# Linear attention and a SwiGLU block on one core: v ahead of the first weights, fewer dummy matmuls, q's casts on two engines

## The chip, the cores and the metric

The kernel runs on one core of one Trainium2 chip. The metric is the device time of one execution in microseconds (us); smaller is better. The tensor engine (TensorE) is called PE below. VectorE is DVE, ScalarE is ACT, GpSimd is POOL, SyncE is SP. POOL issues the loads, and SP issues the first load of q and most of the stores.

## The reference

```python
# q, k, v: (8 batches, 8 heads, 576 positions, 64); phi(x) = elu(x) + 1
kv  = einsum('bhsd,bhse->bhde', phi(k), v);  z = sum over s of phi(k)
x   = einsum('bhsd,bhde->bhse', phi(q), kv) / (einsum('bhsd,bhd->bhs', phi(q), z) + 1e-6)
# heads side by side: x becomes (4608 tokens, 512)
out = (silu(x @ w_gate) * (x @ w_val)) @ w_out        # w_gate, w_val 512 x 1536; w_out 1536 x 512
```

## The kernel before

The work is nine groups of 512 tokens. For each group PE runs layer 1 (96 matmuls of 512 columns, line 290) and layer 2 (48 of them, line 297); attention for the next batches is slipped in between. The attention of batch 0 has nothing to hide behind. It is a chain of short steps at the start, and dummy matmuls (`warm`) fill PE's waits so that its clock rises. That chain, and the order of the first loads, are what the change touches. In the code, `kv` is summed up by PE in PSUM (the tiles named `pp`) and copied out as R; Zr is the same for z. The `corners` are the small matmuls of R and Zr with phi(q): with R they give the numerators of x, with Zr the denominators.

```python
    WARM = (34, 14, 16, 7, 3, 3, 2)
    # [cut]
    def warm(n, w=1, ps=None):      # n dummies of 128*w columns; each is a weight load and a matmul
        for _ in range(n):
            nc.tensor.matmul(out=(ps or pp4[2][1])[:, 256:256 + P * w], lhsT=ones[:, :],
                             rhs=ones[:, :].unsqueeze(1).to_broadcast([P, w, P]), start=True, stop=True)
    # [cut]  kv_corner: 36 matmuls of 64x64; corners: 4 matmuls of up to 512 columns; zt: 9 of 2 columns
    nc.sync.dma_start(out=q32[:, :, :], in_=q[0]...[:, 0:2, :])    # half of q, fp32, quick queue
    ld(q, qr, 0, 1)                                                # the other half, cast by the DMA
    ld2(k, kr, 0)
    ld(v, vr, 0, 0)
    ld_w1(0, 256, 0, 2)
    ld(v, vr, 0, 1)
    ld_w1(0, 256, 2, 4)
    # [cut]  more weights, then:
    ld_w2(0, 4); ld(q, qr, 1, 0); ld_w2(4, 8); ld(q, qr, 1, 1); ld_w2(8, 12); ld2(v, vr, 1)
    # [cut]  the chain, in the order of the program
    for l in range(2):
        nc.vector.tensor_copy(out=qr[0][:, l, :], in_=q32[:, l, :])
    warm(WARM[0])
    for lp in range(2):
        qtr(0, lp, pq[lp])          # 16 transposes of q on PE
        warm(WARM[1 + lp])
        ph[lp][0]()                 # exp on ACT
    # [cut]  exp, max, min of k; z matmuls (zt); Zr; first Zr corners; first k.v; R copy
    zr_copy(0, 1, pp4[3][1])
    warm(WARM[5], 2, pp4[1][1])
    t_corners(0, R, 0, pp4[0])      # numerators of the first four heads
    x_t(0, 0, pp4[0], (0,))         # DVE multiplies: x
    t_corners(0, Zr, 1, pp4[3])     # denominators of the other four heads
    lnrd(pp4[3], 1)
    x_t(0, 0, pp4[0], (1,))
    warm(WARM[6], 2, pp4[1][1])
    l1_mm(0, 0, pp4[2], (0,))
    kv_corner(0, 1, kp, True, False)   # second k.v
    kv_corner(0, 1, ek, False, True)
    r_copy(0, 1, 2, "VV")
    l1_mm(0, 1, pp4[0], (0,))
    t_corners(0, R, 1, pp4[1])
    x_t(0, 1, pp4[1])
    for c in (1, 2, 3):             # twelve layer-1 matmuls without a break
        l1_mm(0, 0, pp4[2], (c,)); l1_mm(0, 1, pp4[0], (c,))
```

Much later, near 81 us, the block for batch 2 issues 144 small k.v matmuls at once and then corners:

```python
            kv_all(b1); r_copy(b1, 0, 2, "AA"); kv_all(b2)        # 2 x 72 matmuls of 64x64
            for lp in range(2):
                corners(kvp[b2], Zr[1], 1, lp, 7, 9, 2 * P + P * lp)
            lnrd(kvp[b2], 0, 2 * P, 4 * P)                        # on ACT
            for lp in range(2):
                num(b1, lp)                                       # R corners
                # [cut]
```

Of the kernel before, what the change touches and what calls it, by code (L numbers as in the profile page):

```python
# [17 lines left out]
def kernel(  # L18
# [10 lines left out]
    nc = tc.nc  # L29
# [10 lines left out]
    EPS = 1e-6  # L40
    SC = 4096.0
    NB = 3
    WARM = (34, 14, 16, 7, 3, 3, 2)

    sb = ctx.enter_context(tc.tile_pool(name="sb", bufs=1))
    pp = ctx.enter_context(tc.tile_pool(name="ps", bufs=1, space=bass.MemoryType.PSUM))
# [2 lines left out]
    def many(shape, dt, name, n=2):  # L49
        return [sb.tile(shape, dt, name=f"{name}_{i}") for i in range(n)]  # L50

    kr = many([P, HL, J * D], FP16, "kr", NB)
    qr = many([P, HL, J * D], FP16, "qr", NB)
    vr = many([P, HL, J * D], FP16, "vr", NB)
# [5 lines left out]
    R = many([P, 2, 2, D], FP16, "R", 3)  # L60
# [4 lines left out]
    q32 = sb.tile([P, 2, J * D], FP32, name="q32")  # L65
# [22 lines left out]
    pp4 = [[pp.tile([P, 512], FP32, name=f"pp_{2 * i + e}") for e in range(2)] for i in range(4)]  # L88
# [11 lines left out]
    def ld(src, dst, b, lp):  # L100
        nc.gpsimd.dma_start(out=dst[b % NB][:, 2 * lp:2 * lp + 2, :],  # L101
                            in_=src[b].rearrange("(l a) (c j) d -> (a c) l (j d)", a=2, j=J)[:, 2 * lp:2 * lp + 2, :])

    def ld2(src, dst, b):
        ld(src, dst, b, 0)
        ld(src, dst, b, 1)

    def ld_w1(f0, f1, c0=0, c1=4):
        for (src, dst) in ((moe_w_gate, wg), (moe_w_val, wv)):
            nc.gpsimd.dma_start(out=dst[:, c0:c1, f0:f1],  # L110
                                in_=src[P * c0:P * c1, f0:f1].rearrange("(c p) f -> p c f", p=P))
# [5 lines left out]
    def act(out, in_, func=AF.Copy, scale=1.0, bias=0.0):  # L117
        nc.scalar.activation(out=out, in_=in_, func=func, bias=bias, scale=scale)  # L118

    def warm(n, w=1, ps=None):  # L120
# [3 lines that stand above are left out]
# [53 lines left out]
    def kv_corner(b, lp, t, first, last):  # L177
        ps = kvp[b]
        for j in range(J):
            for l2 in range(2):  # L180
                for hh in range(2):
                    rows = slice(C * hh, C * hh + C)
                    nc.tensor.matmul(out=ps[hh][D * l2:D * l2 + D, D * lp:D * lp + D],  # L183
                                     lhsT=t[b % 2][rows, lp, j, D * l2:D * l2 + D],
                                     rhs=vr[b % NB][rows, 2 * lp + l2, D * j:D * j + D],
                                     start=(first and j == 0), stop=(last and j == J - 1))
# [6 lines left out]
    def r_copy(b, l0, l1, engs):  # L193
        for hh in range(2):
            src = kvp[b][hh][:, D * l0:D * l1].rearrange("p (l d) -> p l d", d=D)
            if engs[hh] == "A":
                act(R[b % 3][:, l0:l1, hh, :], src)
            else:
                nc.vector.tensor_copy(out=R[b % 3][:, l0:l1, hh, :], in_=src)
# [38 lines left out]
    def units(g):  # L238
        us = [(u // J, u % J) for u in range(U * g, U * g + U)]
        res = []  # L240
        for b in sorted(set(u[0] for u in us)):
            js = [j for (bb, j) in us if bb == b]
            res.append((b, js[0], js[-1] + 1, C * us.index((b, js[0]))))
        return us, res
# [3 lines left out]
    def corners(ps, W, b, lp, j0, j1, c0):  # L248
        for l2 in range(2):
            rows = slice(D * l2, D * l2 + D)  # L250
            for hh in range(2):
                nc.tensor.matmul(out=ps[l2][C * hh:C * hh + C, c0:c0 + C * (j1 - j0)],  # L252
                                 lhsT=W[rows, lp, hh, :], rhs=qt(b, lp, hh, j0, j1)[rows],
                                 start=True, stop=True)
# [16 lines left out]
    def l1_mm(g, fb, ps, chunks):  # L271
        for c in chunks:
            for h, w in enumerate((wg, wv)):
                nc.tensor.matmul(out=ps[h][:, :], lhsT=w[:, c, P * fb:P * fb + P], rhs=xT[g % 2][:, c, :],  # L274
                                 start=(c == 0), stop=(c == 3))
# [36 lines left out]
    def l2_out(g, t, eng, n0=0, n1=512, o=None):  # L312
# [8 lines left out]
        for e in range(2):  # L321
# [9 lines left out]
                      in_=q[0].rearrange("(l a) (c j) d -> (a c) l (j d)", a=2, j=J)[:, 0:2, :])  # L331
    ld(q, qr, 0, 1)
    nc.gpsimd.iota(out=idx[:, :], pattern=[[-1, P]], base=0, channel_multiplier=1)
    ld2(k, kr, 0)
    ld(v, vr, 0, 0)
    ld_w1(0, 256, 0, 2)
    ld(v, vr, 0, 1)
    ld_w1(0, 256, 2, 4)
    ld_w1(256, 512)
    ld_w1(512, 768)  # L340
# [23 lines left out]
    def qtr(b, lp, ps):  # L364
        pt = ps[:, :].bitcast(FP16).rearrange("p (j c) -> p j c", c=P)
        for j in range(J - 1):
            for l2 in range(2):
                nc.tensor.transpose(out=pt[D * l2:D * l2 + D, j, :], in_=qr[b][:, 2 * lp + l2, D * j:D * j + D],  # L368
                                    identity=id16[:, :])
# [14 lines left out]
    def t_phi_main(b, lp, ps):  # L384
        return t_phi(qT[b][:, lp, 0:8, :, :].rearrange("p j h c -> p (j h c)"), ps[:, :].bitcast(FP16))
# [5 lines left out]
    def zt(b, lp, ps, t, first, last):  # L391
        for j in range(J):
            nc.tensor.matmul(out=ps[:, 0:2], lhsT=t[b % 2][:, lp, j, :], rhs=ob[:, 0:P:C],  # L393
                             start=(first and j == 0), stop=(last and j == J - 1))

    def zr_copy(b, lp, ps):
        nc.vector.tensor_scalar(out=Zr[b][:, lp, :, :], in0=ps[:, 0:2].unsqueeze(2).to_broadcast([P, 2, D]),
                                scalar1=1.0 / SC, scalar2=None, op0=ALU.mult)

    def lnrd(ps, i, w0=0, w1=512):  # L400
        for l2 in range(2):
            act(lnt[2 * i + l2][:, w0:w1], ps[l2][:, w0:w1], AF.Ln, bias=epsb[:, 0:1])
            act(rd[i][:, l2, w0:w1], lnt[2 * i + l2][:, w0:w1], AF.Exp, scale=-1.0)

    def xmul(dst, ps, r):
        nc.vector.scalar_tensor_tensor(out=dst, in0=ps, scalar=1.0 / SC, in1=r, op0=ALU.mult, op1=ALU.mult)  # L406

    def x_t(g, lp, ps, l2s=(0, 1)):
        for l2 in l2s:
            xmul(xT[g % 2][:, 2 * lp + l2, :], ps[l2][:, :], rd[lp][:, l2, :])  # L410

    def t_corners(g, W, lp, ps):
        for (b, j0, j1, c0) in units(g)[1]:
            corners(ps, W[b], b, lp, j0, j1, c0)

    def t_add_half(lp, ps, h):
        a = qT[0][:, lp, 4 * h:4 * h + 4, :, :].rearrange("p j h c -> p (j h c)")
        nc.vector.scalar_tensor_tensor(out=a, in0=ps[:, 256 * h:256 * h + 256].bitcast(FP16), scalar=0.0, in1=a,
                                       op0=ALU.max, op1=ALU.add)
# [1 line left out]
    pq = pp4[0]  # L421
    kvp[0] = pp4[1]
    ph = [t_phi_main(0, lp, pq[lp]) for lp in range(2)]
    for l in range(2):
        nc.vector.tensor_copy(out=qr[0][:, l, :], in_=q32[:, l, :])  # L425
    warm(WARM[0])
    for lp in range(2):
        qtr(0, lp, pq[lp])
        warm(WARM[1 + lp])
        ph[lp][0]()  # L430
# [5 lines left out]
    zt(0, 0, pp4[3][0], kp, True, False)  # L436
    warm(WARM[3], 2)
    ph[1][1]()
# [3 lines left out]
    zr_copy(0, 0, pp4[3][0])  # L442
    warm(WARM[4], 2)
    t_corners(0, Zr, 0, pp4[2])
# [6 lines left out]
    zt(0, 1, pp4[3][1], ek, False, True)  # L451
    r_copy(0, 0, 1, "VV")
    t_add_half(1, pq[1], 1)
    zr_copy(0, 1, pp4[3][1])
    warm(WARM[5], 2, pp4[1][1])
    t_corners(0, R, 0, pp4[0])
    x_t(0, 0, pp4[0], (0,))
    t_corners(0, Zr, 1, pp4[3])
    lnrd(pp4[3], 1)
    x_t(0, 0, pp4[0], (1,))  # L460
    warm(WARM[6], 2, pp4[1][1])
    l1_mm(0, 0, pp4[2], (0,))
    kv_corner(0, 1, kp, True, False)
    kv_corner(0, 1, ek, False, True)
    r_copy(0, 1, 2, "VV")
    l1_mm(0, 1, pp4[0], (0,))
    t_corners(0, R, 1, pp4[1])
    x_t(0, 1, pp4[1])
# [254 lines left out]
```

## Time and profile before

| | before |
|---|---|
| time, median of the first 3 executions | 316.74 us (316.49 to 316.79) |
| span of the profiled execution | 315.4 us |
| share of the chain of waits on PE | 96% |
| twelve unbroken layer-1 matmuls begin | 18.35 us (18.42 in the chain) |

PE is the bound from about 18 us to the end.

The chain of waits of the kernel before, in order of time (start us, length us, what held the end of the program):

```profile
4.38 1.14 DVE qr L425 x2
...
5.56 1.06 PE pp L368 x14
6.62 1.61 PE pp L122 x14
8.23 1.02 PE pp L368 x9
...
14.17 0.35 DVE R L199 x2
...
14.57 0.49 PE pp L122 x3
15.05 0.35 PE pp L252 x2
...
16.84 0.71 PE pp L183 x72
...
18.42 2.74 PE pp L274 x12
...
81.42 1.55 PE pp L183 x144
82.97 0.71 PE pp L252 x17
83.67 2.69 PE pp L297 x12
```

Dummies (L122) stand on the chain at 6.62 and 14.57, where they delay useful work. And near 81 us the 144 small matmuls (L183), the corners (L252) and layer 2 (L297) follow one another without a hole; the corners take 0.71 us.

### The profile page before, as it was taken

Reading aid. Unit: us, or ns where it says so; the run is one execution under the profiler, and the core shown is the slowest. Engines: PE = TensorE matmul, PEld = TensorE weight load, DVE = VectorE, ACT = ScalarE, POOL = GpSimd, SP = SyncE. Lnnn points to the kernel's source line nnn. Section 1 sums busy time; section 2 is a strip of 40 time slices with the busy share of each in tenths; the row PEclk is TensorE's granted clock in tenths of the full one; section 3 lists DMA queues with packets and bytes.
Section 4 is the critical chain, followed back from the end, with each engine's and each line's share of the span. In section 5 each row is a group of like instructions: output and inputs, shape, how many; then the busy total and the mean of one; then the engine's idle time right before and its main releaser. Section 6 shows DMA issues by size and latency. Waiting matters only on the chain.

```text
span 315.4 us, 5768 instructions
## 1 busy us (share of the span) xinstructions
PE 309.3 (98%) x2311; PEld 148.5 (47%) x2311; DVE 204.5 (65%) x354; ACT 151.2 (48%) x228; POOL 48.3 (15%) x73
## 2 busy tenths in 40 slices
PE   8999999999999999999999999999999999999994
PEld 7744444444544454445444544445444444444442
DVE  2754867999689676978598749874991434134410
ACT  2765849638653655357434743475331333133311
POOL 7655344300000230014000500000000000000000
PEclk9999999999999999999999999999999999999999
DMA  7999999997612297129803890314022400140014
GB/s 154 198 198 199 206 207 225 244 207 106 139 33 41 48 166 183 30 47 148 213 4 72 125 236 1 76 30 105 2 53 59 98 1 1 35 100 0 0 35 100
DMA packets 41163, 32.52 MB, mean 103 GB/s; under 512 B 16432, under 2 KB 36400, under 8 KB 41136
## 3 DMA queue, kind: packets, MB, share of 16 engines
q0 software_dynamic: 20736, 18.58, 37.9%
q1 hardware_dynamic: 20320, 13.54, 18.4%
q8 instruction: 18, 0.29, 0.4%
q14 instruction: 9, 0.07, 0.1%
q10 hardware_dynamic: 80, 0.03, 0.0%
HBM read 37.75 MB, written 9.44 MB: 150 GB/s over the span
## 4 chain that ended last, share of the span: by engine, by line
PE 96%; DMA 1%; DVE 1%; ACT 1%; issue 0%; DVEq 0%
PE pp L290 57%; PE pp L297 30%; PE pp L274 2%; PE pp L252 2%; PE pp L183 2%; DMA q<-in_q_dram 1%; PE pp L368 1%; PE pp L122 1%; DVE qr L425 0%; ACT ek L118 0%; ACT qT L118 0%; PE pp L393 0%; DVE xT L406 0%; PE pp L210 0%; DVE osb L320 0%
## 5 line engine op out<-in xcount | busy, mean ns | idle before, releaser
L118 ACT ACTIVATE sil<-pp 128x512 f16<-128x512 f32 x108 | 63.4, 597 | 102.0 <-PE pp L290 94.3
L290 PE MATMUL pp<-xT,wg 128*128 128x512 f16 x416 | 106.8, 379 | 0.0
L290 PE MATMUL pp<-xT,wv 128*128 128x512 f16 x416 | 106.8, 379 | 0.0
L283 DVE SCALAR_TENSOR_TENSOR hT<-pp,sil 128x512 f16<-128x512 f32 x108 | 72.2, 680 | 46.8 <-PE pp L290 34.9
L297 PE MATMUL pp<-wo,hT 128*128 128x512 f16 (+2 forms) x444 | 97.0, 374 | 0.6 <-DVE osb L320 0.6
L297 PEld LDWEIGHTS <-hT 128*128 128x128 f16 x444 | 41.9, 98 | 49.9 <-issue 2.1
L290 PEld LDWEIGHTS <-wv 128*128 128x128 f16 x416 | 40.6, 98 | 49.2
L290 PEld LDWEIGHTS <-wg 128*128 128x128 f16 x416 | 40.6, 98 | 48.5
L320 DVE TENSOR_SCALAR osb<-pp 128x512 f32<-128x512 f32 (+1 forms) x19 | 12.9, 681 | 32.7 <-PE pp L297 32.7
L118 ACT ACTIVATE osb<-pp 128x512 f32<-128x512 f32 (+1 forms) x18 | 10.2, 572 | 34.3 <-PE pp L297 34.3
L118 ACT ACT_TABLE_LOAD x13 | 16.7, 1283 | 2.3 <-PE pp L290 2.1
L118 ACT ACTIVATE ek<-kr 128x1152 f16<-128x1152 f16 x16 | 17.7, 1154 | 0.1
L657 POOL COPY gate<-qT 128x1 f16<-128x1 f16 x4 | 1.2, 305 | 97.9 <-DMA qT<-qp 70.2
L227 DVE TENSOR_TENSOR qp<-qp,rden 128x1152 f16<-128x1152 f16 x12 | 16.2, 1347 | 0.0
L218 DVE TENSOR_REDUCE den<-prod 128x18 f32<-128x1152 f16 x12 | 16.1, 1342 | 0.0
L269 DVE TENSOR_SCALAR xT<-pp 128x512 f16<-128x512 f32 (+1 forms) x14 | 8.8, 666 | 7.7 <-PE pp L252 7.7
L118 ACT ACTIVATE eq<-qr 128x1152 f16<-128x1152 f16 x12 | 13.2, 1147 | 0.0
L101 POOL DMA_DIRECT2D vr<-in_v_dram x16 | 11.7, 734 | 8.3 <-PE pp L290 3.1
L101 POOL DMA_DIRECT2D kr<-in_k_dram x16 | 11.5, 722 | 8.1 <-DMA vr<-in_v_dram 3.6
L101 POOL DMA_DIRECT2D qr<-in_q_dram x15 | 11.0, 734 | 7.2 <-DMA wo<-in_moe_w_out_dram 1.8
L145 DVE TENSOR_SCALAR ek<-ek 128x1152 f16<-128x1152 f16 x16 | 8.1, 508 | 5.7 <-ACT ek L118 5.7
L157 DVE TENSOR_TENSOR kp<-ek,kp 128x1152 f16<-128x1152 f16 x14 | 10.6, 758 | 0.5
(68 smaller groups left out, 189.5 us busy)
## 6 DMA issues: line engine op xcount, KB each, us to landing
out_dram<-osb SPq DMA_DIRECT2D x70, 128.0 KB, 3.7
kr<-in_k_dram POOLq DMA_DIRECT2D x16, 288.0 KB, 8.6
vr<-in_v_dram POOLq DMA_DIRECT2D x16, 288.0 KB, 9.9
qr<-in_q_dram POOLq DMA_DIRECT2D x15, 288.0 KB, 11.7
wo<-in_moe_w_out_dram POOLq DMA_DIRECT2D x3, 512.0 KB, 13.0
wg<-in_moe_w_gate_dram POOLq DMA_DIRECT2D x5, 256.0 KB, 9.7
wv<-in_moe_w_val_dram POOLq DMA_DIRECT2D x5, 256.0 KB, 10.3
q<-in_q_dram SPq DMA_DIRECT2D x1, 576.0 KB, 3.6
```

The source lines that it names most:

```text
L101: nc.gpsimd.dma_start(out=dst[b % NB][:, 2 * lp:2 * lp + 2, :], in_=src[b].rearrange("(l a) (c j) d -> (a c) l (j d)", a=2, j=J)[:, 2 * lp ...
L118: nc.scalar.activation(out=out, in_=in_, func=func, bias=bias, scale=scale)
L145: nc.vector.tensor_scalar(out=a, in0=a, scalar1=1.0, scalar2=None, op0=ALU.min)
L157: nc.vector.tensor_tensor(out=a, in0=ek[b % 2][:, lp, :, :], in1=a, op=ALU.add)
L183: nc.tensor.matmul(out=ps[hh][D * l2:D * l2 + D, D * lp:D * lp + D], lhsT=t[b % 2][rows, lp, j, D * l2:D * l2 + D], rhs=vr[b % NB][rows, 2 ...
L218: nc.vector.tensor_reduce(out=den[:, c, :], in_=prod[:, :, :].rearrange("p j (l d) -> p (j l) d", d=D), axis=AX.X, op=ALU.add)
L227: nc.vector.tensor_tensor(out=qv, in0=qv, in1=rden[:, c, :].unsqueeze(2).to_broadcast([P, 2 * J, D]), op=ALU.mult)
L269: nc.vector.tensor_scalar(out=dst, in0=ps[l2][:, c0:], scalar1=1.0 / SC, scalar2=None, op0=ALU.mult)
L283: nc.vector.scalar_tensor_tensor(out=hT[g % 2][:, fb, :], in0=ps[1][:, :], scalar=SC, in1=s[:, :], op0=ALU.mult, op1=ALU.mult)
L290: nc.tensor.matmul(out=ps[h][:, :], lhsT=w[:, c, P * fb:P * fb + P], rhs=xT[g % 2][:, c, :], start=(c == 0), stop=(c == 3))
L297: nc.tensor.matmul(out=l2p[(g, t)][:, n0:n1], lhsT=hT[g % 2][:, fb, P * t:P * t + P], rhs=wo[:, fb, n0:n1], start=(fb == 0), stop=(fb == F ...
L320: nc.vector.tensor_scalar(out=o[:, n0:n1], in0=ps[:, n0:n1], scalar1=1.0 / SC, scalar2=None, op0=ALU.mult)
```

## The change

The intent: load all of v of batch 0 before the weights so that its second k.v can run before the first layer-1 matmul; run fewer dummies while PE is cold, that is, at half clock, since each then takes about 107 ns; cast q on DVE and ACT at once; and put the first R corners ahead of the three wide dummies.

```diff
-    WARM = (34, 14, 16, 7, 3, 3, 2)
+    WARM = (32, 8, 8, 6, 3, 3)
@@
     ld(v, vr, 0, 0)
+    ld(v, vr, 0, 1)
     ld_w1(0, 256, 0, 2)
-    ld(v, vr, 0, 1)
@@
-    for l in range(2):
-        nc.vector.tensor_copy(out=qr[0][:, l, :], in_=q32[:, l, :])
+    nc.vector.tensor_copy(out=qr[0][:, 0, :], in_=q32[:, 0, :])
+    act(qr[0][:, 1, :], q32[:, 1, :])
@@
+    t_corners(0, R, 0, pp4[0])
     zr_copy(0, 1, pp4[3][1])
     warm(WARM[5], 2, pp4[1][1])
-    t_corners(0, R, 0, pp4[0])
-    x_t(0, 0, pp4[0], (0,))
     t_corners(0, Zr, 1, pp4[3])
     lnrd(pp4[3], 1)
-    x_t(0, 0, pp4[0], (1,))
-    warm(WARM[6], 2, pp4[1][1])
-    l1_mm(0, 0, pp4[2], (0,))
+    x_t(0, 0, pp4[0], (0,))
     kv_corner(0, 1, kp, True, False)
     kv_corner(0, 1, ek, False, True)
+    x_t(0, 0, pp4[0], (1,))
     r_copy(0, 1, 2, "VV")
+    l1_mm(0, 0, pp4[2], (0,))
     l1_mm(0, 1, pp4[0], (0,))
```

The change removes 19 dummies (2 of 34, 6 of 14, 8 of 16, 1 of 7 and the last 2) and no other work of PE; it moves the rest.

## The prediction

> **What bounds the kernel now.** The chain of waits is 96% PE: from about 18.4 us to the end PE runs dense matmuls (two-layer feed-forward) with no wait worth naming; the table of PE waits has one of 0.6 us, near the end. The clock column reads full speed. So the only thing this change can move is the moment at which the dense phase begins. In the timeline, twelve of the first 16 layer-1 matmuls run without a break from 18.35 us; everything before is a chain of short steps with dummies between them.
>
> **That chain before (timeline and chain).** q lands 4.35; two DVE casts end 5.51 (0.46 and 0.75); 16 transposes end 6.62; 14 dummies hold PE to 8.2; 16 transposes to 9.25; ACT exp of qT 9.27 to 10.29; exp of k 1.15; min on DVE 11.37; z matmuls 11.89; Zr copy; Zr corners 12.66; first k.v 13.3 to 14.1; R copy to 14.52; three wide dummies, which wait for that copy, 14.57; R corners 14.98; x multiply 15.50; second k.v only at 16.8; R copy 17.6; R corners 18.01; dense 18.35.
>
> **What each part is worth.**
> 1. Cast split: DVE 0.46 beside ACT (estimate 0.65 us, from ACT's 0.60 at 512 and 1.15 at 1152 columns): both done about 5.05, so -0.45 us. Second transposes then wait for q's other half, landed about 7.6 to 7.8 (issued 1.24, 6.3 us to landing), so they start about 7.75, not 8.16. 14 to 8 dummies is what lets this through (107 ns each cold: -0.64 us of PE). Net on exp of k: -0.4 us.
> 2. 16 to 8 dummies: z matmuls then wait for DVE's max on k, not for PE. No further gain.
> 3. R corners ahead of the three dummies: -0.4 us, partly hidden, as DVE still owes an add (0.68) and the Zr copy (0.28) before the x multiply.
> 4. v's second half moves two 128 KB transfers ahead: landing about 13.4 instead of 14.7 to 15.0. Second k.v can run right after the second Zr corners, about 15.4 instead of 16.8; its R copy is then bound by DVE's two x multiplies (about 16.7 instead of 17.95). The first weights land 1.4 us later (about 14.0 and 14.7), still before their matmuls at about 16.1.
>
> Adding these along the chain: dense phase about 17.35 instead of 18.35: **-1.0 us** if PE's clock behaves as before. Later weights have margin: they land at least 1.5 us ahead of use (worst: columns 1024 on), so no new DMA wait.
>
> **The clock.** Dummy spacing (about 105 ns until 8.2, 56 to 110 ns per 128 or 256 columns after 10.1) says that PE became fast near 10.1 us; the clock column doesn't show it. The Trainium skill, "TensorE: Matmul & The Clock Gate", Part 1, says the array starts at half clock and is released after one busy window of about 3.4 us; its window is free-running. Before, 6.6 to 10.1 was nearly full of work. After, PE idles about 0.8 us there and runs 14 dummies fewer. If release slips to about 13.5, z matmuls, wide dummies and Zr corners run at half speed: an estimated +0.5 to +1.0 us back. I give that 35%.
>
> **Prediction.** 316.0 us (-0.7), range 315.2 to 316.8. Faster by over 2%: 1%; within 2%: 98%; slower by over 2%: 1%.
>
> **What would show it.** Right: second transposes near 7.75, first R corners near 14.2, second k.v near 15.4, twelve unbroken layer-1 matmuls from 17.3 to 17.6, the rest unchanged. Wrong: wide dummies or z matmuls at twice their spacing after 10.1 us; a wait of PE on weights; dense phase at 18 or later.
>
> **What would make it wrong.** A late clock release, a table load before ACT's cast, or first weights later than 16 us.

## More of the kernel before

Most executions of this kernel lie within half a microsecond of each other, but some are 1 to 3 us longer.

The page's summary of the kernel before: each digit is one fortieth of the span in tenths busy; `PEclk` is the granted clock in tenths; the last two lines are the chain that ended last, by engine, and the transfers of the queue that the profile calls "instruction".

```profile
PE   8999999999999999999999999999999999999994
PEclk9999999999999999999999999999999999999999
PE 96%; DMA 1%; DVE 1%; ACT 1%; issue 0%; DVEq 0%
...
q8 instruction: 18, 0.29, 0.4%
```

## The result and the profile after

The changed kernel took 318.96 us in the median of 4 executions (318.08 to 319.19), the kernel before 316.71 us of 4 (316.49 to 316.79). The ratio is 1.0067, with a 95% interval of 1.0047 to 1.0087. It is slower, by under 1%. Ratios here are the mean time of one kernel's fast runs over that of the other's of the same rounds, so they are not quite the ratios of the medians quoted.

| | before | after |
|---|---|---|
| span of the profiled execution, us | 315.4 | 317.1 |
| twelve unbroken layer-1 matmuls begin (chain) | 18.42 | 17.81 |
| first full layer-1 block of group 0 (chain) | 21.16 | 20.54 |
| last layer-2 block near 84 us begins (chain) | 83.67 | 85.39 |

So the dense phase began 0.6 us earlier in this profile, and between 20.5 and 85.4 us the kernel lost 2.3 us. How much of the 0.6 us is the edit's is less sure than it looks, because the first rise of the clock is recorded at 10.24 us in the one profile and at 4.71 in the other; the section on why the prediction was wrong comes back to it. The same lines of the page for the changed kernel:

```profile
PE   6999999999799999999999999999999999999994
PEclk9799999999999999999999999999999999999998
PE 94%; DMA 2%; ACT 1%; DVE 1%; issue 1%; POOLq 0%
...
q8 instruction: 18, 0.29, 0.4%
```

The 7 in PE's row, in the eleventh slice (79 to 87 us), is new. The 7 in the clock's row (8 to 16 us) is a spell at half clock. The chain of waits of the changed kernel:

```profile
7.83 0.85 PE pp L368 x16
...
13.69 0.35 DVE R L199 x2
14.03 0.61 DVE qT L418
...
14.68 0.40 PE pp L252 x2
15.09 0.43 PE pp L122 x3
15.52 0.34 PE pp L252 x4
15.86 0.64 PE pp L183 x72
...
17.81 2.74 PE pp L274 x12
...
80.80 1.52 PE pp L183 x144
82.33 0.38 PE pp L252 x7
82.71 0.46 ACT lnt L118
...
84.01 0.42 ACT rd L118
84.43 0.33 issue
84.76 0.63 PE pp L252 x16
85.39 2.70 PE pp L297 x12
```

At the start the R copy is 0.48 us earlier (13.69, not 14.17), but the second half of the R corners now waits for DVE's add (14.03 to 14.64), because it writes the PSUM bank that this add still reads. The three wide dummies follow, and the second Zr corners begin at 15.45 in the timeline, no earlier than before (15.37). What this profile wins at the start it wins behind them, by running the second k.v at once (15.86, not 16.84).

At 82 us there is a hole of 2.3 us between the Zr corners and the R corners, and the chain fills it with ACT's logarithm and exponential. The table of PE's waits of the changed kernel puts it down to ACT too:

```profile
PE pp L252 <- ACT rd L118: 2.3, 1, 2.3
```

That name is wrong. The program has PE wait here for the two R copies on ACT and for q's DMA transposes; ACT's `rd` is not among them. In the kernel before, whose program is the same here, the R corners began at 82.89, and `rd` was not done until 85.06. The timelines of the two kernels, of ACT and of PE's weight loads (start, length, instruction), first the kernel before:

```profile
82.21 0.45 ACT L118 ACTIVATE R<-pp 128x128 f16<-128x128 f32 x2 [0.15 <-PE pp L183]
...
82.76 0.16 PEld L252 LDWEIGHTS <-Zr 64*64 64x64 f16 x8
...
82.88 0.53 PEld L252 LDWEIGHTS <-R 64*64 64x64 f16 x16
```

And the changed kernel:

```profile
81.59 0.45 ACT L118 ACTIVATE R<-pp 128x128 f16<-128x128 f32 x2 [0.16 <-PE pp L183]
...
82.12 0.16 PEld L252 LDWEIGHTS <-Zr 64*64 64x64 f16 x8
...
84.76 0.36 PEld L252 LDWEIGHTS <-R 64*64 64x64 f16 x16 [2.48 <-ACT rd L118]
```

In the changed kernel the R copies were done at 82.05, and the transposes' semaphores were full at 76.17 and 80.36. Everything that the program waits for was there, and even the first weight load of R did not start for 2.5 us. What differs is the transfer of the queue named "instruction". The DMA view of the kernel before, from 77 to 78.5 us (transfers, MB, share):

```profile
q8 instruction: 1, 0.02, 3.9%
```

The DMA view of the changed kernel has none there; it has one from 81 to 82.5 us, next to the stores of group 1:

```profile
q1 hardware_dynamic: 176, 0.30, 91.0%
q8 instruction: 1, 0.02, 5.3%
```

In the trace this transfer of 16,384 bytes starts at 77.87 before and at 82.05 after (and takes 0.93 and 1.27 us). Each kernel has 18 of them. The Trainium skill, page "Runtime: NRT & Kernel Launch", section "Instruction fetch mechanics", says that an engine's instruction store is a FIFO refilled in 16 KiB blocks of 256 instructions by a DMA queue of its own, and that the cost is mostly hidden. Eighteen blocks are 4,608 instructions, which fits PE's 4,635 here; that the cost is hidden is in doubt.

**The theory.** A block of PE's program used to be fetched in the dense stage, 3.5 us before the burst of 144 small matmuls (288 instructions in 1.5 us). With 38 instructions fewer, the same point in PE's stream comes later: the dense stage takes two instructions per 0.216 us, so an estimate from the trace is 38 x 0.108 = 4.1 us later, less the 0.6 us won, so 3.5; the trace shows 4.2. That puts the fetch inside the burst, which uses up the instructions at hand before the next block has come. **Rivals:** the R corners' own inputs or the stores that now run 0.6 us earlier; the clock, which reads half speed for a while near 10 us; the new order itself.

### The profile page after: what moved, and what is told of

It is laid out like the page before. It is cut to its first block, busy times and chain, and to the rows that moved or that the text cites. A ratio compares the mean times of both kernels' runs of the same rounds, so it can differ in the third digit from the quotient of the medians.

```text
span 317.1 us, 5730 instructions
## 1 busy us (share of the span) xinstructions
PE 307.3 (97%) x2292; PEld 146.2 (46%) x2292; DVE 203.6 (64%) x353; ACT 152.0 (48%) x229; POOL 48.2 (15%) x73
## 4 chain that ended last, share of the span: by engine, by line
PE 94%; DMA 2%; ACT 1%; DVE 1%; issue 1%; POOLq 0%
PE pp L290 57%; PE pp L297 30%; PE pp L274 2%; PE pp L252 2%; DMA qr<-in_q_dram 2%; PE pp L183 2%; PE pp L368 1%; ACT ek L118 0%; ACT qT L118 0%; ACT lnt L118 0%; PE pp L210 0%; DVE kp L141 0%; DVE qT L418 0%; DVE osb L320 0%; DVE ek L145 0%
```

## Experiments

All were correct, and each batch ran on one chip with the kernel before beside it (11 executions per batch). "Full clock" means a mean granted clock of 0.997 or more over an execution. This mean counts only from the first record of the clock, so a PE that never sped up early is not seen in it.

| run | median us | before us | ratio (95%) | executions at full clock: mean | before at full clock |
|---|---|---|---|---|---|
| e1_pad19 | 316.88 | 316.54 | 1.0013 (0.9976 to 1.0050) | 3 of 6: 315.91 | 316.57 |
| e2_before_minus19 | 319.58 | 316.54 | 1.0083 (1.0055 to 1.0110) | 3 of 6: 318.61 | 316.57 |
| e3_pad10 | 316.59 | 316.54 | 1.0008 (0.9976 to 1.0040) | 3 of 6: 316.28 | 316.57 |
| e4_minus16 | 320.46 | 316.54 | 1.0116 (1.0077 to 1.0155) | 1 of 6: 318.80 | 316.57 |
| e5_refill | 317.25 | 317.15 | 1.0013 (0.9975 to 1.0052) | 3 of 6: 316.28 | 316.76 |
| e6_refill_no3 | 316.90 | 317.15 | 1.0015 (0.9980 to 1.0050) | 3 of 6: 316.65 | 316.76 |
| e7_thin_before | 316.44 | 317.15 | 0.9994 (0.9957 to 1.0030) | 5 of 6: 316.35 | 316.76 |
| e8_casts_only | 316.67 | 317.15 | 0.9992 (0.9966 to 1.0018) | 5 of 6: 316.64 | 316.76 |
| e9_order_only | 316.48 | 316.80 | 0.9996 (0.9968 to 1.0025) | 5 of 6: 316.31 | 316.62 |
| e10_refill_no3_qfirst | 315.59 | 316.80 | 0.9964 (0.9943 to 0.9984) | 6 of 6: 315.56 | 316.62 |
| e11_changed_again | 319.92 | 316.80 | 1.0109 (1.0083 to 1.0136) | 1 of 6: 319.06 | 316.62 |
| e12_casts_qfirst | 316.08 | 316.80 | 0.9983 (0.9964 to 1.0003) | 6 of 6: 316.19 | 316.62 |
| e13_thin_all | 319.03 | 316.47 | 1.0071 (1.0054 to 1.0089) | 3 of 6: 319.19 | 316.57 |
| e14_refill_again | 317.59 | 316.47 | 1.0025 (0.9996 to 1.0053) | 3 of 6: 316.52 | 316.57 |
| e15_best_again | 315.80 | 316.47 | 0.9989 (0.9957 to 1.0022) | 3 of 6: 315.61 | 316.57 |

### e1_pad19: the changed kernel with PE's program as long as before

```diff
+    def tiny(n):                     # dummies of two columns
+        for _ in range(n):
+            nc.tensor.matmul(out=pp4[2][1][:, 256:258], lhsT=ones[:, :], rhs=ones[:, 0:2], start=True, stop=True)
@@ in the loop over lp, where PE waits for q's other half
         warm(WARM[1 + lp])
+        tiny(19 if lp == 0 else 0)
```

> The changed kernel with 19 tiny dummy matmuls (two columns each) put into PE's idle time before the second transposes, so that PE's program has as many instructions as the kernel before (38 more than the changed one). Theory (supply of PE's instructions): the 16 KB block of PE's program that was fetched at 82.05 us, in the middle of a burst of 288 short instructions, is again fetched near 77 us, before the burst; the 2.6 us hole in PE at 82.2 us is gone and the start's gain of 0.6 us is left: 316.1 us, ratio to before 0.998. Rival (the hole comes from output writes and transposes that now run 0.6 us earlier): the hole stays, 318.9 us. Rival (PE's clock): time stays within 0.3 us of 318.9.

The hole is gone: the R corners follow the Zr corners by 0.12 us (85.05, 85.17). Nothing but 19 two-column dummies at 6 us was added, and neither stores nor inputs of the corners were touched. Adding work made the kernel faster, which the rivals named above do not explain: in the three executions at full clock the mean is 315.91 us, 0.66 under the kernel before. The other three took 318.5 us in the mean, at a mean clock of 0.984 to 0.993. The profiled execution was one of those; its clock by stretch of time (length, PE busy, granted clock, DMA share, GB/s):

```profile
7.50:10.90 3.40, 3.40 (x39) 0.50 1.19 196
10.90:14.30 3.40, 2.73 (x108) 0.99 1.34 195
14.30:21.20 6.90, 6.90 (x94) 0.51 1.42 198
```

PE's clock fell to half twice, the second time across the beginning of the dense phase. So there is a second loss, of another kind, which is in some executions only.

### e2_before_minus19: the kernel before with 38 PE instructions fewer

```diff
-    warm(WARM[0])
+    warm(WARM[0] // 2, 2)            # 34 narrow dummies as 17 wide ones
@@
-        warm(WARM[1 + lp])
+        warm(WARM[1 + lp] - 4 * lp)
+        warm(2 * lp, 2)              # 4 narrow ones as 2 wide ones
```

> The kernel before, with 38 narrow dummies written as 19 of twice the width: same dummy time, 38 PE instructions fewer, nothing else changed. Theory: a hole of 2 to 2.6 us in PE appears just before the R corners near 82.8 us, with the fetch of an instruction block inside the burst before it: 318.9 to 319.3 us, ratio 1.007 to 1.008. Rivals (earlier start, order of v, casts): no hole, 316.7 us.

The converse holds. With the old order, the old casts and the same dummy time, the hole is there, with an instruction transfer at 81.76. PE's timeline:

```profile
81.91 0.30 PE L252 MATMUL pp<-qT,Zr 64*64 64x128 f16 x8
84.78 0.41 PE L252 MATMUL pp<-qT,R 64*64 64x384 f16 x8 [2.57 <-ACT rd L118]
```

The time is 2.0 us above the kernel before at full clock; the other three executions, at a mean clock of 0.991 or 0.992, took 320.2 us. Neither the new order nor the casts are needed for the hole; the length of PE's program is.

One rival is left by this run alone: its dense phase began at 17.48, 0.87 us earlier than in the profile of the kernel before, with the clock's first rise at 5.49 instead of 10.24. A later run rules that rival out. e12_casts_qfirst, whose PE program has its full length, also began the dense phase at 17.48 and the burst at 80.48, as this run did. Its PE shows no hole:

```profile
81.93 0.47 PE L252 MATMUL pp<-qT,Zr 64*64 64x128 f16 x8
82.20 0.64 PE L252 MATMUL pp<-qT,R 64*64 64x384 f16 x16
```

### e3_pad10: half the padding

The edit is that of e1_pad19 with `tiny(10 ...)`.

> The changed kernel with 10 tiny dummies (20 PE instructions more than the changed one, 18 fewer than before). Theory: in the dense stage PE takes 20 instructions in 2.1 us, so the block is asked for about 2.1 us earlier than in the changed kernel and the hole shrinks from 2.6 to about 0.5 us: 316.6 us (316.3 to 317.0). If the size of the hole doesn't depend on the position in this way (all or nothing), 316.1 or 318.9.

The transfer is at 79.76, 2.3 us earlier than in the changed kernel, as the estimate had it. There is no hole before the corners. The burst itself is about 0.2 us longer (80.61 to 82.22 until the Zr corners, 1.61 us; the kernel before took 1.43 from 81.35 to 82.78). So the direction is right and the 0.5 us expected was too much. The hole does not shrink microsecond for microsecond.

### e4_minus16: 32 PE instructions fewer still

```diff
-    warm(WARM[0])
+    warm(WARM[0] // 2, 2)            # in the changed kernel: 32 narrow ones as 16 wide ones
```

> The changed kernel with its first 32 narrow dummies written as 16 wide ones: 32 PE instructions fewer still. Theory: the missing block now begins 32 instructions later in the program, after the R corners, at the first output matmul of the next group; it is asked for a little later, inside the burst, and PE needs it about 0.7 us later: the hole moves behind the R corners and is 1.8 to 2.3 us, time 318.2 to 318.8 us. If the hole belongs to the R corners themselves (their inputs), it stays in front of them at 2.6 us.

The hole moved, as expected, from in front of the R corners to behind them, 32 instructions later in the program. PE's timeline:

```profile
84.92 0.30 PE L252 MATMUL pp<-qT,Zr 64*64 64x128 f16 x8
85.04 0.71 PE L252 MATMUL pp<-qT,R 64*64 64x384 f16 x16
87.25 0.60 PE L297 MATMUL pp<-wo,hT 128*128 128x512 f16 x2 [1.50 <-issue]
```

From the R corners' start to layer 2 it is 2.21 us, and 0.72 before, so the hole is 1.5 us; 1.8 to 2.3 was expected. Here the profile itself says "issue": PE waited for nothing that it shows. The R corners' inputs are thereby ruled out. In all four profiles with a hole (the changed kernel, this run, e2_before_minus19, e11_changed_again), 1,729 recorded PE instructions come before it: it keeps its place in PE's stream, whatever work stands there. The median of 320.46 us is mostly clock: five of six executions were at 0.981 to 0.989.

### e5_refill and e14_refill_again: full dummies put back into the idle time

```diff
-    WARM = (32, 8, 8, 6, 3, 3)
+    WARM = (32, 23, 12, 6, 3, 3)
```

> The changed kernel with 19 full dummies put back (15 in PE's idle time before the second transposes, 4 after them): PE program as long as before and PE as busy as before in the first 10 us. Two causes are claimed for the loss: the hole near 82 us (position of an instruction block) and a clock that falls back to half at 8 to 21 us in some executions because PE has idle time there. Expected: no hole, clock column full after about 10 us, no executions with a mean clock under 0.99; 316.0 us with the spread of the kernel before (most runs within 0.5 us), ratio 0.998. If the clock's fall doesn't come from the thinned dummies, some executions stay at 317 to 319 us with a mean clock under 0.99.

> The refilled kernel once more: 3 of its 6 executions had a mean clock of 0.989, while the kernel with the new order alone and the one with the early q load had none in 6 each. If the new order with its casts loses windows in a good part of executions: 2 or more of 6 at 0.990 or less again. If that was chance of one chip or hour: none or one.

There was no hole, and the dense phase began at 17.53 in e5_refill's profile. But the clock still fell: 5 of the 12 executions of the two runs had a mean clock of 0.990 or less. My reason for the fall, that the thinned dummies of the first 10 us caused it, is therefore not enough. In the profile of e14_refill_again PE stood 0.87 us for v's first half at 12.1 to 13.0 and was at half clock from 14.6 to 18.0.

### e6_refill_no3: the three wide dummies out of the chain

```diff
-    WARM = (32, 23, 12, 6, 3, 3)
+    WARM = (32, 23, 15, 6, 3, 0)     # against e5_refill
```

> As the refilled kernel, with the three wide dummies between the first R corners and the second Zr corners moved to the start (as three narrow ones), so that PE's program keeps its length. In the changed kernel Zr corners start at 15.45, though Zr is ready at 14.83 and PE free at about 15.03; the dummies stand in between. Expected: Zr corners at about 15.05, dense phase 0.4 us earlier, 315.6 us. If DVE's multiplies hold the chain instead, 0 to 0.1 us.

The Zr corners came at 14.49 and the dense phase at 16.78, 0.75 us earlier than in e5_refill's profile. Most of this did not reach the time, because a new wait stood at 40 us. From the table of PE's waits of this run:

```profile
PE pp L376 <- DMA qr<-in_q_dram: 0.8, 1, 0.8
```

These are the transposes of q of batch 1. In the kernel before its second half landed at 40.80 and was used at 41.67, so there were 0.87 us to spare. Of the 1.57 us by which this profile began the dense phase earlier than the kernel before's (16.78, not 18.35), 0.54 were left after the wait (the chain has layer 2 at 41.99, not 42.53). The prediction checked the first-layer weights and missed this load.

### e7_thin_before and e13_thin_all: thinner dummies alone

```diff
-        warm(WARM[1 + lp])
+        warm(8)                      # e7_thin_before
+        tiny(WARM[1 + lp] - 8)
```

In e13_thin_all every dummy after the first 34 becomes `tiny`. Program length and order are those of the kernel before.

> The kernel before with 14 of its narrow dummies (6 before the second transposes, 8 after) cut from 128 columns to 2: program, order and length as before, PE only less busy between 6 and 10.5 us. If thinning alone lets the clock fall: no hole, but in a third or more of the executions a mean clock under 0.99 and 317.5 to 319.5 us, the others 316.3 (second transposes about 0.3 us earlier). If thinning doesn't touch the clock: all near 316.3 us, spread as before.

> The kernel before with every dummy after the first 34 cut to 2 columns (program, order and length as before, PE much less busy from 6 to 18 us). If PE's idleness after the first dummies is what lets the clock fall, nearly all executions lose windows: 4 or more of 6 with a mean clock of 0.993 or less, some at 0.985, 317.5 to 321 us. If the clock's fall is chance that the dummies after the first don't touch, the shares stay as for the kernel before (about 1 of 5 at 0.993 or less, none at 0.990) and the time is near 316.3 us.

Thinning 14 dummies lost clock windows in one execution of six (0.988, 319.52 us), which decides nothing. Thinning all later ones cost time in six of six: three had a mean clock of 0.983 or 0.984 and took 317.9 to 318.9 us (in the profile of one the clock is at half from 8.6 to 18.8 us), and three took 319.1 to 319.3 us with a mean clock of 1.000. In the latter the clock cannot be read from the mean; a first release that came late would look like this, but none of these three was profiled. That the dummies after the first 34 are worth about 2.5 us together is shown by the times; how the loss divides is not.

### e8_casts_only, e9_order_only: the two parts by themselves

e8_casts_only is the kernel before with the two cast lines of the change. e9_order_only is the changed kernel with both casts on DVE and `WARM = (34, 14, 18, 7, 3, 3)`; PE's program is as long as before in both.

> The kernel before with q's casts on two engines alone; PE's program is the same. Casts done 0.45 us earlier, first transposes end 0.45 us earlier, the 14 dummies behind them end near 7.75, where q's other half lands: the chain moves 0.35 to 0.4 us, dense phase 17.95 to 18.0, 316.3 us, ratio 0.999. If the chain had slack there, 316.7 us. No hole either way.

> The changed kernel's order of loads and of PE's work with casts on DVE alone and as many narrow dummies as the kernel before (PE program as long as before). Time in executions with a mean clock of 0.997 or more: the R corners' second half waits for DVE's add, then three wide dummies, so Zr corners near 15.9 and dense phase near 18.2: 316.3 to 316.6 us, gain of 0.1 to 0.3 us. Clock: so far 14 of 34 executions of kernels with the new order have a mean clock of 0.990 or less (two windows or more at half clock), and none of 38 with the old order and full dummies. If the order does it, 2 or more of 6 here; if the casts or the dummies do it, none.

At full clock the casts give 0.1 us (316.64 against 316.76) and the order 0.3 us (316.31 against 316.62). Both intervals of the ratio include 1. The expected starts of the dense phase were missed: 17.95 to 18.0 and 18.2 were expected, the profiles have 16.96 and 17.14, with the clock's first rise at 5.45 and 6.83 instead of the 10.24 of the kernel before. In both profiles PE waited for q of batch 1 near 40 us (0.3 and 0.4 us). Neither kernel had an execution at 0.990 or less.

### e10_refill_no3_qfirst, e15_best_again, e12_casts_qfirst: the load of q of batch 1 earlier

```diff
     ld(q, qr, 1, 0)
-    ld_w2(4, 8)
     ld(q, qr, 1, 1)
+    ld_w2(4, 8)
```

e10_refill_no3_qfirst and e15_best_again are e6_refill_no3 with this edit; e12_casts_qfirst is e8_casts_only with it.

> The refilled kernel without the three wide dummies waited 0.8 us at 40 us for the second half of q of batch 1 and so gave back what it had won. Here that load goes ahead of the 512 KB load of output weights before it (landing about 2.6 us earlier). Expected: no wait at 40 us, 315.5 to 315.7 us in executions with a mean clock of 0.997 or more (0.9 us under the kernel before); executions with a fallen clock (about a third) 317 to 318.5. If something else holds PE at 40 us, 316.5 us.

> The best kernel once more, to see whether it holds on another occasion: executions with a mean clock of 0.997 or more 315.1 to 316.0 us; ratio under 1 with the interval mostly below it if at most one execution loses clock windows, about 1.000 if three do.

> The kernel before with the casts on two engines and the second half of q of batch 1 loaded ahead of the output weights before it. Casts alone had the dense phase 1 us earlier in its profile but waited 0.3 us for that load. Expected: no wait at 40 us, 315.7 to 316.2 us in executions with a mean clock of 0.997 or more, at most 1 of 6 with a clock of 0.990 or less; ratio 0.997 to 0.999. If the casts' gain is not real, 316.6 us.

The wait at 40 us is gone in the profile of e10_refill_no3_qfirst (span 314.0 us). Its six executions took 315.1 to 316.0 us, and the ratio is 0.9964 with the interval below 1. On the second occasion four were at 315.2 to 316.0 us and two, at a clock of 0.989, at 317.5 and 318.6. When the clock holds, this version beats the kernel before by 1.0 us on either occasion (315.56 against 316.62, 315.61 against 316.57). It is not proof against the clock, and on the second occasion the interval of its ratio includes 1. e12_casts_qfirst took 315.9 to 316.6 us, with no lost window.

### e11_changed_again: the changed kernel once more

> The changed kernel once more, beside the others on one chip. Hole theory: every execution is longer than 317.9 us; those with a mean clock of 0.997 or more 318.1 to 319.2 us; those with one or more windows at half clock 319 to 322 us. Ratio 1.007 to 1.012. If the first result was chance of the chip or of its clock alone, some executions at 316.1 us.

All six executions were at 319.06 us or more, and its profile has the hole again (PE 2.30 us before the R corners, instruction transfer at 82.30). PE also waited 0.2 us for q of batch 1. Five of six were below full clock, so its median is 1 us worse than in the first result.

## Why the prediction was wrong

It put the time at 316.0 us in a range of 315.2 to 316.8; 318.96 was measured.

- **The step that failed:** "So the only thing this change can move is the moment at which the dense phase begins." It also named "the rest unchanged" as the sign of being right. Taking 38 instructions out of PE's stream moved the fetch of an instruction block at 77.87 us into a burst at 82.05 us and cost 2.3 us. That the length of PE's program makes the hole is shown from both sides: with the length restored the hole is gone (e1_pad19, e5_refill), with 38 fewer in the old kernel it is there (e2_before_minus19; e12_casts_qfirst has the same times up to the burst, the full length, and no hole), and with 32 fewer still it moves 32 instructions on (e4_minus16). That PE stood for want of instructions is inferred from the transfer's place in the burst and from the absence of any other wait.
- **The gain at the start was not confirmed at its size.** Predicted was -1.0 us on the clock as before; the two profiles differ by 0.6 (17.81 against 18.42), but their clocks differ too. With the start's work of the kernel before and a first rise at 5.49 (e2_before_minus19) the dense phase began at 17.48; the changed kernel, with a rise at 4.78 and no fall (e11_changed_again), began it at 17.60. So these profiles do not show how much of the 0.6 us is the edit's. At full clock and with the program's length restored, the times are under the kernel before by 0.66 us (e1_pad19), 0.48 (e5_refill) and 0.05 (e14_refill_again). One term is seen to be mis-sized: "R corners ahead of the three dummies" implied Zr corners at about 15.0, and they came at 15.45, because the R corners' second half waited for DVE's add on the same PSUM bank and the three dummies then still stood in front of them. Second transposes "near 7.75" came at 7.83; first R corners "near 14.2" at 13.96, half of them at 14.68; second k.v "near 15.4" at 15.7.
- **"No new DMA wait" held only by luck of size.** In the changed kernel's first profile there was none. q of batch 1 had 0.87 us to spare in the kernel before, and in four profiles that began the dense phase earlier PE waited for it: the changed kernel itself 0.2 us in e11_changed_again, e8_casts_only 0.3, e9_order_only 0.4 and e6_refill_no3 0.8. The full 1.0 us would have been cut.
- **The clock risk was real, but not as told.** The prediction feared a release at 13.5 us instead of 10.1. In the profiled execution the clock rose early and fell again. The granted clock of the changed kernel by stretches of time:

```profile
0.00:4.70 4.70, 3.60 (x32) 1.00 0.55 139
4.70:8.10 3.40, 1.63 (x34) 1.00 1.12 169
8.10:11.50 3.40, 3.28 (x43) 0.50 1.20 201
11.50:15.00 3.50, 3.19 (x110) 1.00 1.39 195
```

  The 1.00 of the first line stands for no record: before the first rise the dummies follow one another at 107 ns. At 5.6 to 6.0 they do so at 56 ns, and at 8.7 to 9.3 at 107 ns again, which agrees with the rise and the fall. The first rise is recorded at 4.71, the fall at 8.12, the next rise at 11.53: steps of 3.41 us, which agrees with the window that the Trainium skill, "TensorE: Matmul & The Clock Gate", Part 1, states (4096 cycles at 1.2 GHz). The second of these stretches had PE busy for 1.63 us. This fall seems to have cost the profiled execution little: the chain then stood mostly with ACT and DVE, and e11_changed_again's profile, without the fall, began the dense phase only 0.14 us earlier (17.60, not 17.74 in the timeline). It costs more where it meets the dense phase, as in e1_pad19. The first rise was at 10.24 us in the profile of the kernel before and anywhere from 3.9 to 7.1 us in the other profiles, so its place differs between executions.

**What stays open.** Executions at a mean clock of 0.990 or less were 19 of 64 for kernels with the new order, and none of 62 for kernels with the old order and all dummies. The bound matters: at 0.993 or less it was 26 of 64 and 9 of 62. Yet order alone had 0 of 6, refilled kernels 5 of 12, and the best kernel 0 of 6 and 2 of 6. That PE's idleness costs clock is supported by e13_thin_all; which wait of the new order costs it is not settled. PE's busy time in a window does not settle it: the changed kernel's clock fell after 1.63 of 3.40 us and e1_pad19's after 2.73, but in e11_changed_again it stayed full after 2.05 (4.8 to 8.2 us), and in e12_casts_qfirst after 2.21 (4.1 to 7.5). Also open is why PE resumes only 1.2 to 1.5 us after the instruction transfer has ended (83.31 and 84.76 in the changed kernel), and at which point a fetch is asked for.

## What to carry to other kernels

A change in the number of an engine's instructions can change the timing far behind the edit, as it did here by 2.3 us: when a long stretch gains or loses time where nothing was edited, look at the instruction transfers and at bursts of short instructions, and test it by padding the program back to its old length. A hole whose named releaser is not among the waits of the program, or is "issue", is a reason to look there. Before a gain at the start is counted in full, look for the next load that has less to spare than the gain.

## What the Trainium skill lacked or had wrong

- "Runtime: NRT & Kernel Launch", "Instruction fetch mechanics": it says that crossing a 16 KiB block is mostly hidden and that issue is slower than the refill. Here a burst of 288 PE instructions in 1.5 us outran it, and PE stood 2.3 to 2.6 us (e2_before_minus19, e11_changed_again and the changed kernel). From the start of the transfer to PE's next instruction it was 2.4 to 3.0 us. The page gives PE's store as 2048 instructions in one sentence and, in another, every store as two blocks; a store with 2048 instructions ahead would not be expected to run dry in a burst of 288. That is an argument for the smaller figure; no run here measures the store.
- "TensorE: Matmul & The Clock Gate", "Why this matters for your kernels", advises against idle gaps above about 3 us. Here the clock fell after a window in which PE was busy for 1.63 of 3.40 us, its longest gap being 1.64 us, and after one busy for 2.73 of 3.40 us (e1_pad19), while in e11_changed_again it stayed full after one busy for 2.05. So a gap under 3 us can be followed by a fall, and no bound on the busy time comes out of these runs. What the page lacks is a figure for idles shorter than this, which it mentions elsewhere for another kernel.
- No page that I found says that the profile puts a hole in instruction supply down to an engine that PE does not wait for. Here it named ACT's `rd` in three profiles (of two kernels: the changed one twice, and e2_before_minus19) and "issue" in one (e4_minus16).
